# Token weights behind batch 0's inputs, fp32 filler matmuls and earlier u transposes in a fused scan and mixer

## The chip, the cores and the metric

The kernel runs on one core of one Trainium2 chip. Times are device microseconds (us) of that core. Most runs of a kernel agree within about one per cent; a run that is over 1.5% above the fastest of the same kernel is called slow and is left out of comparisons. The span of a profiled execution is about 2 us shorter than the device time of that execution (189.9 of 192.06 us for the kernel before), so spans are compared only with spans.

## The reference

```python
# recurrent part: B=4, H=8, S=768, D=48
state = alpha[t][:, None] * state + outer(k[t], v[t])
y[t]  = q[t] @ state
# y becomes x with shape (4, 768, 384); then a token and channel mixer
h  = relu(x^T @ w_tok1) @ w_tok2          # 768 -> 256 -> 768, over tokens
u  = x + h^T
h2 = relu(u @ w_ch1) @ w_ch2              # 384 -> 1536 -> 384, over channels
out = u + h2
```

Inputs and output are fp32; q, k, v and alpha come to 18.9 MB together.

## The kernel before

The sequence of each batch is cut into 6 chunks of 128 steps, so there are 24 chunks, n = 0 to 23. A chunk needs a logarithm of alpha, a cumulative sum on TensorE, two exponentials, products with k (GpSimd) and q (VectorE), transposes, scores, a mask product and the output y. When a batch's six chunks are done, its mixer runs: token products 1 and 2, u, transposes of u, 72 matmuls of channel product 1, and the same number of channel product 2. The mixer of one batch is interleaved with the chunks of the next.

A small scheduler of the program's own, `Plan`, simulates the engines with assumed durations and thereby fixes the order in which each engine gets its instructions. The chip then follows that order, whatever the real times are.

```python
class Plan:
    LAG = {"PE": 220, "ACT": 180, "DVE": 150, "POOL": 110}
    def op(self, engines, emit, deps=(), prio=0, takes=None, frees=(), lands=0.0): ...
    def issue(self):
        # ... takes the earliest possible operation, and of equals the lower prio
        slow = 2.0 if e == "PE" and start < self.cold else 1.0
        # ... models of the wire: `heavy` for weights, `wire` for inputs
        o["emit"](eng)

    inp = pool("inp", NIN)                                   # NIN = 6
    u128 = consts.tile([128, 128], BF16, name="u128")
    id128 = consts.tile([128, 128], BF16, name="id128")
    ones_col = consts.tile([128, 1], BF16, name="ones_col")
    # ... fix, wpool

    def load(n, name, src, after=None):                      # at, kt, qt, vt
            c[name] = inp.tile([128, H, D], F32, name=name)
            nc.sync.dma_start(c[name], src[b, :, ci * C : ci * C + C, :].transpose([1, 0, 2]))

    def weight(name, dst, src, after, us):                   # fp32 in DRAM, bf16 in SBUF
            gps.dma_start(dst, src)

    # state of the scan, in a ring of three buffers
    s_prev = ss_t[(n - 1) % NSS]                             # NSS = 3
    # e_ss (made for 5 of the 6 chunks of a batch) writes ss_t[n % NSS]

    for n in range(NT):                                      # NT = 24, NCH = 6
        # ... load_ak, load_qv, chunk(n)
        if n == NCH - 2:
            weight("wt1", wt1, src1, acqm, 2.6)
        if n == NCH - 1:
            weight("wt2", wt2, src2, pkk, 2.3)
            weight_ch1(0, vb); weight_ch1(1, vb); weight_ch1(2, vb)
        if n == NCH:
            weight_ch2(0, vb)
        if n == NCH + 1:
            weight_ch2(1, vb)
        # ... loads of chunk n + 1; mixer(b - 1) at the end of batch b
```

## Time and profile before

| | kernel before |
|---|---|
| device time, median of 3 runs | 193.34 us (192.79 to 193.99) |
| span of the profiled execution | 189.9 us (one of 192.06 us), mean granted clock 0.964 |
| TensorE busy | 168.6 us, 89% of the span |
| first matmul of channel product 1, batch 0 | 41.09 us |
| first and last matmul of channel product 2, batch 0 | 57.5 us and 75.5 us |
| last input used (logarithm of chunk 23) | 115.5 us |

The windows view of the kernel before gives for each stretch of time its length, the busy time and the number of instructions of TensorE (PE), its weight loads (PEld), VectorE (DVE), ScalarE (ACT) and GpSimd (POOL), the granted clock, the busy share of the DMA engines and the rate that they moved:

```profile
core 0: us, PE busy (x) PEld busy (x) DVE busy (x) ACT busy (x) POOL busy (x), PEclk, DMA share, GB/s
0.00:38.00 38.00, 23.36 (x238) 15.27 (x239) 19.77 (x42) 13.27 (x27) 16.16 (x34) 0.82 1.02 179
5.00:20.00 15.00, 9.70 (x111) 6.84 (x111) 10.31 (x14) 6.92 (x16) 6.98 (x12) 1.00 1.13 218
20.00:30.00 10.00, 5.50 (x70) 3.80 (x69) 5.44 (x9) 2.27 (x5) 5.86 (x10) 0.65 0.96 150
30.00:45.00 15.00, 14.08 (x102) 8.02 (x103) 7.12 (x13) 5.91 (x13) 2.54 (x5) 0.78 1.06 184
38.00:58.00 20.00, 19.42 (x189) 12.14 (x188) 10.26 (x18) 15.54 (x34) 9.35 (x14) 1.00 1.15 205
58.00:78.00 20.00, 20.00 (x236) 13.04 (x235) 13.04 (x20) 8.58 (x20) 11.17 (x18) 1.00 1.01 199
78.00:118.00 40.00, 37.33 (x480) 25.56 (x479) 27.98 (x44) 29.46 (x65) 24.94 (x39) 1.00 1.01 212
```

TensorE has no gap in 58 to 78 us, and gaps of 2.7 us in 78 to 118 us. In 20 to 30 us it is busy 5.50 of 10 us, and in 30 to 45 us it is busy but on average at 0.78 of its clock. The DMA share adds up the times of the packets on 16 engines, and so it can exceed 1.

The timeline of the kernel before shows start and duration, engine, line, operation, what is written and read, and in brackets the idle time before it and what ended that. Here are chunk 5's q product and the first of the channel matmuls:

```profile
28.03 0.56 DVE L283 TENSOR_TENSOR pkq_126<-qt,a_sb 128x384 bf16<-128x384 f32 x1 [2.46 <-DMA qt<-in_q_dram]
```

```profile
41.09 2.11 PE L474 MATMUL ps_mm<-ut,wc_156 128*128 128x384 bf16 x12 [0.28 <-DVE ut L455]
```

### The profile page before, as it was taken

What the parts mean: (1) busy time and instruction counts of PE and PEld (TensorE: products, weight loads), DVE (VectorE), ACT (ScalarE), POOL (GpSimd) and SP (SyncE); (2) the same over time, 40 slices, a digit from 0 to 9 for tenths busy, and PEclk for the clock granted to TensorE, in tenths of its full rate; (3) what the DMA queues carried; (4) which work ended last, traced back from release to release, by engine and by line L of the source; (5) the groups of instructions that cost most, each with busy time, mean ns of one, the idle gap of its engine ahead of it and who ended that gap; (6) DMA issues with size and microseconds to landing.
All of it is one profiled execution on the core that took longest, in us unless ns stands there. A gap on an engine that the chain in (4) does not pass through costs nothing.

```text
span 189.9 us, 4180 instructions
## 1 busy us (share of the span) xinstructions
PE 168.6 (89%) x1616; PEld 107.5 (57%) x1616; DVE 90.9 (48%) x152; ACT 93.7 (49%) x200; POOL 64.2 (34%) x108
## 2 busy tenths in 40 slices
PE   1377467989999999999979999999999999999992
PEld 0255344456666666657736676655665666566651
DVE  2378547172725676669734896323717102220222
ACT  3534411339885333677777588400664990059000
POOL 3643546006925555795535655500000000000000
PEclk9999955699999999999999999999999999999999
DMA  6999799999999999999999997022200001220122
GB/s 124 226 204 216 143 175 146 198 182 224 191 217 197 195 221 195 200 237 210 243 228 208 190 198 159 2 83 86 83 0 3 0 0 61 104 87 0 59 107 85
DMA packets 107139, 27.00 MB, mean 142 GB/s; under 512 B 100336, under 2 KB 107120, under 8 KB 107120
## 3 DMA queue, kind: packets, MB, share of 16 engines
q1 hardware_dynamic: 103296, 23.60, 58.1%
q0 software_dynamic: 3824, 3.15, 11.1%
q8 instruction: 12, 0.20, 0.4%
q14 instruction: 7, 0.06, 0.1%
HBM read 25.17 MB, written 4.72 MB: 157 GB/s over the span
## 4 chain that ended last, share of the span: by engine, by line
PE 70%; SPq 11%; DMA 8%; issue 3%; POOL 3%; DVE 2%; ACT 2%; POOLq 0%; DVEq 0%; ACTq 0%
PE ps_mm L492 25%; PE ps_mm L474 21%; SPq L230 11%; PE ps_mm L402 5%; PE ps_mm L426 4%; DMA qt<-in_q_dram 3%; PE gt_ps L324 3%; DMA vt<-in_v_dram 2%; DMA at<-in_alpha_dram 2%; PE ps_y L362 2%; PE ps_tp L307 2%; PE ps_mm L447 2%; PE ps_tp L312 2%; PE ps_y L367 1%; POOL pkk_131 L279 1%
## 5 line engine op out<-in xcount | busy, mean ns | idle before, releaser
L384 ACT ACTIVATE rt<-ps_mm 128x384 bf16<-128x384 f32 x90 | 43.2, 491 | 30.2 <-PE ps_mm L474 29.6
L474 PE MATMUL ps_mm<-ut,wc_156 128*128 128x384 bf16 x288 | 54.4, 326 | 0.3 <-DVE ut L455 0.3
L492 PE MATMUL ps_mm<-wc_157,rt 128*128 128x384 bf16 x288 | 49.7, 326 | 0.0
L492 PEld LDWEIGHTS <-rt 128*128 128x128 bf16 x288 | 27.3, 98 | 17.3 <-issue 0.2
L330 DVE TENSOR_TENSOR gtm<-gt_ps,u_107 128x1024 bf16<-128x1024 f32 x24 | 29.3, 1221 | 10.8 <-PE gt_ps L324 10.8
L474 PEld LDWEIGHTS <-wc_156 128*128 128x128 bf16 x288 | 25.9, 97 | 14.8 <-issue 0.8
L504 DVE TENSOR_TENSOR o_sb<-ps_mm,u_sb 128x384 f32<-128x384 f32 x24 | 13.4, 556 | 42.2 <-PE ps_mm L492 41.3
L317 DVE COPY tp<-ps_tp 128x1024 bf16<-128x1024 bf16 x21 | 14.4, 688 | 14.1 <-PE ps_tp L312 13.1
L291 POOL CAST vb<-vt 128x384 bf16<-128x384 f32 x24 | 12.1, 504 | 25.3 <-DMA vt<-in_v_dram 19.4
L375 ACT ACTIVATE x_sb<-ps_y 128x384 bf16<-128x384 f32 x24 | 11.8, 490 | 14.0 <-PE ps_y L367 13.8
L270 ACT ACTIVATE ia_sb<-ps_cum 128x384 f32<-128x384 f32 x24 | 11.8, 491 | 11.7 <-PE ps_cum L264 11.7
L433 DVE TENSOR_TENSOR u_sb<-ps_mm,x_sb 128x384 bf16<-128x384 f32 x24 | 11.8, 550 | 5.2 <-PE ps_mm L426 5.2
L402 PE MATMUL ps_mm<-x_sb,wt_154 128*128 128x384 bf16 x48 | 12.3, 375 | 0.0
L275 ACT ACTIVATE a_sb<-ps_cum 128x388 f32<-128x388 f32 x24 | 11.9, 495 | 0.0
L426 PE MATMUL ps_mm<-ht,wt_155 128*128 128x384 bf16 x48 | 10.6, 328 | 0.6 <-DVE u_sb L433 0.3
L279 POOL TENSOR_TENSOR pkk_131<-kt,ia_sb 128x384 bf16<-128x384 f32 x6 | 6.3, 1048 | 14.2 <-ACT ia_sb L270 14.2
L324 PE MATMUL gt_ps<-tp 48*128 48x128 bf16 x192 | 10.4, 233 | 0.6 <-DVE tp L317 0.4
L362 PE MATMUL ps_y<-vb,gtm 128*128 128x48 bf16 x192 | 9.3, 189 | 1.4 <-DVE gtm L330 1.4
L362 PEld LDWEIGHTS <-gtm 128*128 128x128 bf16 x192 | 8.2, 100 | 3.4 <-DVE gtm L330 2.0
L324 PEld LDWEIGHTS <-tp 48*128 48x128 bf16 x192 | 6.0, 99 | 6.2 <-issue 3.7
L279 POOL TENSOR_TENSOR pkk_130<-kt,ia_sb 128x384 bf16<-128x384 f32 x6 | 6.0, 997 | 8.8 <-ACT ia_sb L270 8.8
L279 POOL TENSOR_TENSOR pkk_129<-kt,ia_sb 128x384 bf16<-128x384 f32 x6 | 6.0, 1002 | 5.5 <-ACT ia_sb L270 5.5
(105 smaller groups left out, 195.5 us busy)
## 6 DMA issues: line engine op xcount, KB each, us to landing
at<-in_alpha_dram SPq DMA_DIRECT2D x24, 192.0 KB, 3.7
kt<-in_k_dram SPq DMA_DIRECT2D x24, 192.0 KB, 3.9
qt<-in_q_dram SPq DMA_DIRECT2D x24, 192.0 KB, 3.8
vt<-in_v_dram SPq DMA_DIRECT2D x24, 192.0 KB, 3.8
out_dram<-o_sb SPq DMA_DIRECT2D x24, 192.0 KB, 1.9
wc_156<-in_moe_w_ch_dram POOLq DMA_DIRECT2D x3, 384.0 KB, 5.9
wc_157<-in_moe_w_ch_dram POOLq DMA_DIRECT2D x2, 576.0 KB, 7.8
wt_154<-in_moe_w_tok_dram POOLq DMA_DIRECT2D x1, 384.0 KB, 6.6
```

Of the source, the lines that this page charges most:

```text
L230: nc.sync.dma_start(c[name], src[b, :, ci * C : ci * C + C, :].transpose([1, 0, 2]))
L279: gps.tensor_tensor(pkk_t[n % NPK][:, :, 0:D], c["kt"], c["ia"], ALU.mult)
L317: (dve.tensor_copy if e == "DVE" else act.copy)(c["tp"], c["ptp"])
L324: pe.matmul(gt[:, 4 * (h % 2) + j, :], lhsT=c["tp"][base : base + D, 4 + j, :], rhs=c["tp"][base : base + D, j, :], start=True, stop=True)
L330: dve.tensor_tensor(c["gtm"], c["gt"], mask_b, ALU.mult)
L362: pe.matmul(ps[:, h, :], lhsT=c["gtm"][:, 4 * (h % 2) + h // 2, :], rhs=c["vb"][:, h, :], start=(h == 0), stop=(ci == 0 and h == H - 1), s ...
L384: act.activation(dst, ps, AF.Relu)
L402: pe.matmul(hold["ps"], lhsT=wt1[:, kc, m * 128 : (m + 1) * 128], rhs=xs[b * NCH + kc], start=(kc == 0), stop=(kc == NS - 1), skip_group_c ...
L426: pe.matmul(hold["ps"], lhsT=wt2[:, kc, i * 128 : (i + 1) * 128], rhs=ht[kc], start=(kc == 0), stop=(kc == NDT - 1))
L474: pe.matmul(hold["ps"], lhsT=wc1[:, kc, mc * 128 : (mc + 1) * 128], rhs=ut_t[0][:, kc, cs], start=(kc == 0), stop=(kc == NM - 1))
L492: pe.matmul(hold["ps"], lhsT=rt[mc][:, i * 128 : (i + 1) * 128], rhs=wc2[:, mc, :], start=(mc == 0), stop=(mc == NDC - 1), skip_group_chec ...
L504: dve.tensor_tensor(hold["o"], hold["ps"], u[i], ALU.add)
```

## The change

The intent is to get batch 0's last chunks, and thus its mixer, started earlier. The first token weight is issued behind chunk 5's work rather than beside its inputs. TensorE's waits in the plan, between 19 and 36.5 us, are filled with matmuls of a constant fp32 tile whose result nobody reads, meant to keep the clock up. The u transposes get a higher priority. Some durations in the plan are refitted. The ring of states is indexed by the number of states made.

```diff
@@ Plan @@
+            if eng == "PE" and self.fill_from < start < self.fill_until:
+                idle = start - max(free[eng], self.fill_from)
+                warm = start > self.cold
+                for _ in range(int(idle * (0.75 if warm else 0.95) / (240.0 if warm else 450.0))):
+                    self.fill()
... (models of the wire: 2900 -> 2400, 1650 -> 1950, partial overlap, a lull; the plan's end of the slow clock: 36 -> 26 us)
@@ kernel @@
+    psy = ps_y_p.tile([128, 512], F32, name="ps_y")
+    def keep_busy():
+        pe.matmul(psy[:, HD:512], lhsT=u32, rhs=u32, start=True, stop=True,
+                  skip_group_check=True)
     u128 = consts.tile([128, 128], BF16, name="u128")
     make_upper_triangular(nc, u128, val=1.0, diag=True)
+    held = consts.tile([128, 1], F32, name="held")
+    u32 = consts.tile([128, 128], F32, name="u32")
+    dve.memset(u32, 1.0)
     id128 = consts.tile([128, 128], BF16, name="id128")
... 
+            if behind is not None:
+                gps.tensor_copy(held, behind["ia"][:, 0, 0:1])
             gps.dma_start(dst, src)
... (channel weights: 2.2 -> 2.8 us, 3.6 -> 4.7 us; RATE 205 -> 214)
... (cum, ia, a, pkk: priority P -> P - 0.3; u transposes and copies: TOK -> TOK - 0.3)
-        s_prev = ss_t[(n - 1) % NSS]
+        s_prev = ss_t[(n - 1 - b) % NSS]
-                    ss_t[n % NSS], ...
+                    ss_t[(n - b) % NSS], ...
         if n == NCH - 2:
-            weight("wt1", wt1, src1, acqm, 2.6)
+            loads[n]["qt"]["lull"] = 1300.0
+            early = vb
         if n == NCH - 1:
-            weight("wt2", wt2, src2, pkk, 2.3)
+            weight("wt1", wt1, src1, ia, 3.4, tiles[n])
+            ia["users"].append((wload["wt1"], None))
+            weight("wt2", wt2, src2, early, 2.9)
```

More of the change, by code (lines that the diff above doesn't have):

```diff
@@ L24, with __init__ @@
     LAG = {"PE": 220, "ACT": 180, "DVE": 150, "POOL": 110}
-    def __init__(self, rings, cold, window, slack):
+    def __init__(self, rings, cold, window, slack, fill, fill_from, fill_until):
+        self.fill, self.fill_from, self.fill_until = fill, fill_from, fill_until
         self.rings = rings
@@ L37, in op @@
         o = {"eng": engines, "emit": emit, "deps": [d for d in deps if d is not None],
-             "prio": (prio, len(self.ops)), "takes": [takes] if isinstance(takes, str) else list(takes or ()), "lands": lands, "users": [],
+             "prio": (prio, len(self.ops)), "takes": [takes] if isinstance(takes, str) else list(takes or ()), "lands": lands, "lull": 0.0, "users": [],
              "end": None}
@@ L57, in issue @@
                 at = max((d["end"] for d in o["deps"]), default=0.0)
-                if "PE" in o["eng"] and at > self.cold:
+                if "PE" in o["eng"] and at > self.fill_until:
                     at = max(d["end"] + (0.0 if "PE" in d["eng"] else self.slack)
@@ L83, in issue @@
             todo.remove(o)
+            if eng == "PE" and self.fill_from < start < self.fill_until:
[3 more added lines that the diff above has]
+                    self.fill()
             free[eng], o["start"] = done, start
             if o["lands"] and eng == "POOL":
-                first = max(heavy, start + 2900.0)
+                first = max(heavy, start + 2400.0)
                 heavy = first + o["lands"]
@@ L90, in issue @@
                 for p in self.ops:
-                    if p["lands"] and p is not o and (p["end"] or 0.0) > first + 900.0 and "SP" in p["eng"]:
-                        p["end"] += o["lands"]
+                    over = (p["end"] or 0.0) - 700.0 - first
+                    if p["lands"] and p is not o and over > 0.0 and "SP" in p["eng"]:
+                        p["end"] += o["lands"] * min(1.0, over / p["lands"])
             elif o["lands"]:
-                wire = max(wire, start + 1650.0) + o["lands"]
-                o["end"] = wire + 900.0
+                wire = max(wire, start + 1950.0) + o["lands"] + o["lull"]
+                o["end"] = wire + 700.0
             else:
@@ L138 @@
     NAUX, NGT, NRT, NMIX = 4, 3, 24, 3
+    FILL_FROM, COLD, FILL_UNTIL = 19000.0, 26000.0, 36500.0
     consts = pool("consts")
@@ L160 @@
                  "gtm": NGT, "ss": NSS, "x": 18, "ht": 4, "u": 12, "ut": 2, "rt": NRT,
-                 "o": 6, "pcum": 1, "ptp": 1, "pgt": 1, "py": 1, "pmix": NMIX}, 36000.0, {"PE": 0.0}, 600.0)
+                 "o": 6, "pcum": 1, "ptp": 1, "pgt": 1, "py": 1, "pmix": NMIX}, COLD, {"PE": 0.0}, 600.0,
+                keep_busy, FILL_FROM, FILL_UNTIL)
     act.preload_act_table_set("natural_log_exp_and_others")
@@ L194, with weight @@
     wload = {}
-    def weight(name, dst, src, after, us):
+    def weight(name, dst, src, after, us, behind=None):
         def emit(e):
+            if behind is not None:
+                gps.tensor_copy(held, behind["ia"][:, 0, 0:1])
             gps.dma_start(dst, src)
@@ L208, in weight_ch1 @@
         cs = slice(g * W1C, g * W1C + W1C)
-        weight(f"wc1{g}", wc1[:, :, cs], src3[:, :, cs], after, 2.2)
+        weight(f"wc1{g}", wc1[:, :, cs], src3[:, :, cs], after, 2.8)
     def weight_ch2(g, after):
         cs = slice(g * W2C, g * W2C + W2C)
-        weight(f"wc2{g}", wc2[:, cs, :], src4[:, cs, :], after, 3.6)
-    RATE = 205.0
+        weight(f"wc2{g}", wc2[:, cs, :], src4[:, cs, :], after, 4.7)
+    RATE = 214.0
     xs = {}
@@ L265, in e_cum @@
                           rhs=ones_col, start=True, stop=True, skip_group_check=True)
-        cum = plan.op({"PE": 260}, e_cum, [ln], P, takes="pcum", frees=[ln])
+        cum = plan.op({"PE": 260}, e_cum, [ln], P - 0.3, takes="pcum", frees=[ln])
         def e_ia(e):
@@ L270, in e_ia @@
             act.activation(c["ia"].rearrange("p h d -> p (h d)"), c["cum"][:, 0:HD], AF.Exp, scale=-1.0)
-        ia = plan.op({"ACT": 375}, e_ia, [cum], P, takes="ia", frees=[cum])
+        ia = plan.op({"ACT": 375}, e_ia, [cum], P - 0.3, takes="ia", frees=[cum])
         def e_a(e):
@@ L275, in e_a @@
             act.activation(c["a"], c["cum"][:, 0 : HD + 4], AF.Exp)
-        a = plan.op({"ACT": 375}, e_a, [cum], P, takes="a", frees=[cum])
+        a = plan.op({"ACT": 375}, e_a, [cum], P - 0.3, takes="a", frees=[cum])
         def e_pkk(e):
             gps.tensor_tensor(pkk_t[n % NPK][:, :, 0:D], c["kt"], c["ia"], ALU.mult)
-        pkk = plan.op({"POOL": 960}, e_pkk, [l_kt, ia], P, takes="pkk", frees=[l_kt, ia])
+        pkk = plan.op({"POOL": 960}, e_pkk, [l_kt, ia], P - 0.3, takes="pkk", frees=[l_kt, ia])
         def e_pkq(e):
@@ L351, in e_ss @@
                 dve.tensor_tensor(
-                    ss_t[n % NSS], c["s"][:, 0:HD].rearrange("p (h d) -> p h d", h=H),
+                    ss_t[(n - b) % NSS], c["s"][:, 0:HD].rearrange("p (h d) -> p h d", h=H),
                     bass.AP(tensor=m.tensor, offset=m.offset,
@@ L359, in e_y @@
         def e_y(e):
-            ps = c["y"] = ps_y_p.tile([128, H, D], F32, name="ps_y")
+            ps = c["y"] = psy[:, 0:HD].rearrange("p (h d) -> p h d", h=H)
             for h in range(H):
@@ L376, in chunk @@
         xop[n] = plan.op({"ACT": 375}, e_x, [y], P, takes="x", frees=[y])
-        return pkk, vb, acqm
+        return pkk, vb, acqm, ia
     xop = {}
@@ L448, in e_utp @@
                                      u[2 * g + i][:, j * 128 : (j + 1) * 128], id128)
-            tj = plan.op({"PE": 330}, e_utp, us[2 * g : 2 * g + 2], TOK,
+            tj = plan.op({"PE": 330}, e_utp, us[2 * g : 2 * g + 2], TOK - 0.3,
                          takes="pmix" if g else ["pmix", "ut"])
@@ L457, in e_ut @@
                     hold["ps"].rearrange("p (j i) t -> p j (i t)", i=2))
-            uts.append(plan.op({"DVE": 470, "ACT": 700}, e_ut, [tj], TOK,
+            uts.append(plan.op({"DVE": 470, "ACT": 700}, e_ut, [tj], TOK - 0.3,
                                frees=[(tj, "pmix")]))
@@ L516 @@
             load_qv(n)
-        pkk, vb, acqm = chunk(n)
+        pkk, vb, acqm, ia = chunk(n)
         if n == NCH - 2:
-            weight("wt1", wt1, src1, acqm, 2.6)
+            loads[n]["qt"]["lull"] = 1300.0
+            early = vb
         if n == NCH - 1:
-            weight("wt2", wt2, src2, pkk, 2.3)
+            weight("wt1", wt1, src1, ia, 3.4, tiles[n])
+            ia["users"].append((wload["wt1"], None))
+            weight("wt2", wt2, src2, early, 2.9)
             weight_ch1(0, vb)
```

## The prediction

> **What bounds it now.** Device time 193.34 us, profiled span 189.9 us. From 50 us on TensorE is nearly saturated: busy time by stretch is 10.00 of 10 us in 50–60, 60–70 and 70–80, 17.6 of 20 in 80–100, 19.7 of 20 in 100–120. The loss lies before the first channel matmul, at 41.09 us (timeline). DMA brings inputs until about 118 us, but TensorE then still has over 60 us of backlog.
>
> Two delays act before 41 us. (1) Batch 0's last q and v: issued at 21.7 and 22.4 us, used at 28.03 and 28.85; the chain of waits has 6.26 us of DMA for that q. The token weight issued at 21.36 us shares the wire: chunk 4's and 5's q and v and that weight are about 1.57 MB in 7.1 us (220 GB/s). VectorE's queue stands behind that q product, so chunk 4's mask product runs at 29.06, though its scores were done at 27. (2) The granted clock is 0.50 from 22.9 to 36.6 us: a 384-column matmul starts every 0.32 us instead of 0.16, and the first token product (31.5–36.2 us) runs wholly so. [...]
>
> **What the change does.** The first token weight goes behind batch 0's last chunk (about 23.5 us instead of 21.4), its data following the inputs. Without that 0.79 MB, the last q and v should land near 25–26 us, 2.5–3 us earlier. The token weights land later (estimate 30 and 33 us instead of 28 and 31.2), just in time. Added: five unread fp32 matmuls, two ahead of chunk 4's y, one before the last token-1 matmuls, two before token-2. [...] With the earlier inputs TensorE should be full from about 28 us, the clock back by 26–33 us. Half of the cold chain from 30 to 36.6 us, at most 3 us, can be saved, overlapping with (1). The earlier u transposes, and a first channel matmul that needs two of three of them, take about 0.5 us more off.
>
> I expect the first channel matmul at about 38.0 us (37–39.5), 3 us earlier. Later the orders change, not the work; saved time survives where TensorE is saturated. Part may go in 80–100 us, where chunk work follows input arrival (2.4 us idle now); earlier channel matmuls could also fill it. Net −3.3 us.
>
> **Predicted: 190.0 us**, 80% range 187.2 to 192.9. Faster by over 2% 0.38, within 2% 0.58, slower by over 2% 0.04.
>
> **Signs.** Right: chunk 5's q product by 26 us; clock 1.0 by 33 us; first channel matmul near 38; the shift still there at the end of batch 1's channel products and at the end. Wrong: clock low until 36 us; token matmuls waiting for weights; idle TensorE at 75–100 us grown by 2–3 us.
>
> **What would make it wrong.** [...] the fixed orders may misjudge when batch 1's inputs land and block on a late tile; or the new order removes more of the 6–7 us that TensorE loses after 41 us (then over 2%).

The forecast's sum came to −3.3 us, from 193.34 to 190.0 us: 3 us at the first channel matmul, and 0.3 us that it does not itemise. The fp32 matmuls had been put within waits.

## More of the kernel before

An input load brings 128 partitions of 8 heads times 48 fp32 values, so it is made of packets of 192 bytes, eight to a partition: the trace of the kernel before holds 98,304 packets of 192 bytes, which is 1,024 for each of the 96 input loads.

In 5 to 20 us, when only inputs are on the wire, 218 GB/s are 17,031 packets of 192 bytes, and 1.13 times 16 engines times 15 us is 271 us: 15.9 ns per packet.

The page's list of DMA issues ends each line with the median time from issue to landing:

```profile
at<-in_alpha_dram SPq DMA_DIRECT2D x24, 192.0 KB, 3.7
```

## The result, and the profile after

| | before | after |
|---|---|---|
| device time, median of 4 runs | 193.06 us (192.62 to 193.99) | 201.38 us (200.93 to 204.38) |
| span of the profiled execution | 189.9 us | 202.4 us |
| first channel-1 matmul, batch 0 | 41.09 us | 41.07 us |
| channel product 2 of batch 0, first and last matmul | 57.5 and 75.5 us | 60.0 and 79.3 us |
| logarithm of chunk 23 | 115.5 us | 125.2 us |

The ratio is 1.042, with a 95% interval of 1.0376 to 1.0464: the change costs 4.2%. Ratios are computed as the mean time of one kernel's fast runs over that of the other's of the same rounds, and so are not quite the ratio of the medians that are quoted. The profiled execution of the kernel after was a slow one of 204.38 us; its fast runs have spans of 198.9 to 199.6 us.

The windows view of the kernel after, for the stretches that were shown of the kernel before:

```profile
core 0: us, PE busy (x) PEld busy (x) DVE busy (x) ACT busy (x) POOL busy (x), PEclk, DMA share, GB/s
5.00:20.00 15.00, 8.73 (x93) 5.92 (x94) 8.04 (x10) 6.21 (x14) 6.98 (x11) 1.00 1.41 187
...
38.00:58.00 20.00, 18.73 (x167) 11.40 (x165) 10.35 (x17) 14.43 (x32) 9.34 (x14) 1.00 1.20 182
58.00:78.00 20.00, 17.31 (x191) 11.53 (x192) 9.85 (x15) 6.82 (x16) 8.25 (x13) 1.00 1.16 189
78.00:118.00 40.00, 34.33 (x428) 22.95 (x426) 23.72 (x33) 25.87 (x59) 22.72 (x35) 0.96 1.14 196
```

The first line is the finding. Already in 5 to 20 us, before the first token weight or filler, the same input loads move at 187 GB/s instead of 218, with a higher share of the DMA engines. By the same estimate as before a packet takes 23.2 ns instead of 15.9. The loss goes on: in 78 to 118 us TensorE is busy 34.33 of 40 us instead of 37.33. For scale, 18.9 MB take 87 us at 218 GB/s and 101 us at 187, an estimate from these two lines; chunk 23's input was seen used 9.7 us later.

The timeline of the kernel after, for chunk 4's and 5's q product, for the last scores of batch 0, which come before the clock rises, and for the first channel matmul:

```profile
26.85 1.05 DVE L304 TENSOR_TENSOR pkq_129<-qt,a_sb 128x384 bf16<-128x384 f32 x1
27.82 0.55 DVE L304 TENSOR_TENSOR pkq_130<-qt,a_sb 128x384 bf16<-128x384 f32 x1
```

```profile
32.46 0.61 PE L345 MATMUL gt_ps<-tp 48*128 48x128 bf16 x8
...
41.07 0.65 PE L495 MATMUL ps_mm<-ut,wc_160 128*128 128x384 bf16 x3 [0.27 <-DVE ut L476]
```

Chunk 5's product, which the prediction had put by 26 us, is at 27.82 us. The scores' eight matmuls take 0.61 us, as at 14.35 us in the kernel before; there they take 0.40 us at 17.47 us, at full clock. So TensorE is still slow at 32.46 us, although the windows view has 1.00 for the clock: the first clock record here is at 34.28 us and raises the clock, and before it the view shows 1.00. In the kernel before the first is at 16.08 us, and the same eight matmuls at 14.35 us were slow under a shown 1.00 too. It is safer to read the clock from the duration of a known matmul.

From the page of the kernel after, the chain that ended last, by engine and by line, and the DMA issue that answers to the one above; then TensorE's waits in 45 to 190 us (in total, times, longest):

```profile
PE 48%; DMA 27%; SPq 7%; issue 7%; POOL 6%; ACT 3%; DVE 0%; POOLq 0%; ACTq 0%
PE ps_mm L513 22%; PE ps_mm L495 15%; DMA at<-in_alpha_dram 13%; SPq L251 7%; DMA kt<-in_k_dram 7%; DMA wc_161<-in_moe_w_ch_dram 5%; DMA wt_159<-in_moe_w_tok_dram 2%; PE ps_mm L423 2%; PE gt_ps L345 1%; POOL vb L312 1%; PE ps_mm L447 1%; PE ps_tp L328 1%; PE ps_mm L468 1%; PE ps_y L383 1%; POOL pkk_133 L300 1%
...
at<-in_alpha_dram SPq DMA_DIRECT2D x24, 192.0 KB, 4.6
```

```profile
PE ps_cum L282 <- ACT la_128 L276: 2.8, 2, 1.6
PE ps_mm L513 <- DMA wc_161<-in_moe_w_ch_dram: 1.8, 1, 1.8
PE ps_cum L282 <- ACT la_125 L276: 1.6, 1, 1.6
PE ps_cum L282 <- ACT la_126 L276: 1.4, 1, 1.4
```

An alpha tile now lands 4.6 us after its issue, not 3.7. In the kernel before, DMA has 8% of that chain (not 27%), and TensorE's waits for logarithms come to 0.7 us in the same stretch, here 5.8. The logarithms (line 276) themselves wait for alpha. The lines of the kernel after are those of before plus 21 in this part.

### The profile page after: what moved, and what is told of

Its sections match the earlier page's. It is cut to its first block, busy times and chain, and to the rows that moved or that the text cites. A ratio compares the mean times of both kernels' runs of the same rounds, so it can differ in the third digit from the quotient of the medians.

```text
span 202.4 us, 4203 instructions
## 1 busy us (share of the span) xinstructions
PE 174.9 (86%) x1626; PEld 112.2 (55%) x1626; DVE 91.9 (45%) x152; ACT 94.3 (47%) x201; POOL 65.5 (32%) x109
## 2 busy tenths in 40 slices
DMA packets 107139, 27.00 MB, mean 133 GB/s; under 512 B 100336, under 2 KB 107120, under 8 KB 107120
## 4 chain that ended last, share of the span: by engine, by line
PE 48%; DMA 27%; SPq 7%; issue 7%; POOL 6%; ACT 3%; DVE 0%; POOLq 0%; ACTq 0%
PE ps_mm L513 22%; PE ps_mm L495 15%; DMA at<-in_alpha_dram 13%; SPq L251 7%; DMA kt<-in_k_dram 7%; DMA wc_161<-in_moe_w_ch_dram 5%; DMA wt_159<-in_moe_w_tok_dram 2%; PE ps_mm L423 2%; PE gt_ps L345 1%; POOL vb L312 1%; PE ps_mm L447 1%; PE ps_tp L328 1%; PE ps_mm L468 1%; PE ps_y L383 1%; POOL pkk_133 L300 1%
## 5 line engine op out<-in xcount | busy, mean ns | idle before, releaser
L495 PE MATMUL ps_mm<-ut,wc_160 128*128 128x384 bf16 x288 | 56.4, 334 | 0.4 <-DVE ut L476 0.3
L495 PEld LDWEIGHTS <-wc_160 128*128 128x128 bf16 x288 | 26.5, 100 | 16.0 <-issue 2.2
L291 ACT ACTIVATE ia_sb<-ps_cum 128x384 f32<-128x384 f32 x24 | 11.8, 493 | 16.6 <-PE ps_cum L285 16.5
L338 DVE COPY tp<-ps_tp 128x1024 bf16<-128x1024 bf16 x19 | 13.0, 686 | 12.6 <-PE ps_tp L333 12.6
L345 PE MATMUL gt_ps<-tp 48*128 48x128 bf16 x192 | 11.0, 243 | 1.7 <-DVE tp L338 1.6
L423 PE MATMUL ps_mm<-x_sb,wt_158 128*128 128x384 bf16 x48 | 11.4, 342 | 0.3 <-ACT rt L405 0.3
```

The lines of the kernel that those rows point to most:

```text
L338: (dve.tensor_copy if e == "DVE" else act.copy)(c["tp"], c["ptp"])
L345: pe.matmul(gt[:, 4 * (h % 2) + j, :], lhsT=c["tp"][base : base + D, 4 + j, :], rhs=c["tp"][base : base + D, j, :], start=True, stop=True)
L423: pe.matmul(hold["ps"], lhsT=wt1[:, kc, m * 128 : (m + 1) * 128], rhs=xs[b * NCH + kc], start=(kc == 0), stop=(kc == NS - 1), skip_group_c ...
L495: pe.matmul(hold["ps"], lhsT=wc1[:, kc, mc * 128 : (mc + 1) * 128], rhs=ut_t[0][:, kc, cs], start=(kc == 0), stop=(kc == NM - 1))
```

## Theories

Where could a slower wire come from at 5 us? The number of packets, 107,139, and the bytes are the same. What did change is where tiles lie. The built program's table of allocations (not a view of the profile) shows it: `held` takes 32 bytes of each partition and `u32` takes 512. Everything allocated behind them has moved by 544 bytes, which is 17 times 32. The input tiles start at byte 56,512 before, a multiple of 64, and at 57,056 after, which is 32 above one.

- *Placement*: the moved input tiles slow the input loads. It has two forms. In one (T1a below), packets that cross a 256-byte boundary cost more. In the other (T1b), packets whose starts aren't multiples of 64 do. Both are guesses that the runs below test.
- *Order*: the new order, or the fillers, cost time by themselves.
- *Lead given back*: once placement is mended, the 3 us gained before the first channel matmul are lost again later, to the wire or to late channel weights.
- *Chance*: the time of the first channel matmul differs from one execution to the next.

The first four kernels below (e1 to e4) were timed on one chip, e5 to e8 on a second, e9 to e12 on a third and e13 to e16 on a fourth; ratios are always to the kernel before on the same chip. The profiled executions of e1 to e8 and e10 to e16 are fast ones, and that of e9 is a single run whose state is unknown.

The texts below number these theories as they came up; each text says what its theories expect.

## The experiments

### Placement: the kernel after moved by another 32 bytes

```diff
-    held = consts.tile([128, 1], F32, name="held")
+    held = consts.tile([128, 16], F32, name="held")[:, 0:1]
```

> The changed kernel with nothing changed but 32 more bytes in its constants (the 4-byte tile that orders the token weight is given 64 bytes), so that all later tiles start at a multiple of 64 bytes again, as before, and not 32 bytes past one. T1 (placement: every input packet lands 32 bytes off in on-chip memory and that slows the input DMA from the first load on): input rate between 5 and 20 us back from 187 to 210-225 GB/s, time 188 to 191 us, that is the 3 us gain that was predicted, ratio to before 0.975-0.99. T2 (the new order and the fixed guesses of arrival cost the time): 199 to 202 us. T3 (the fp32 matmuls cost it): 199 to 202 us.

Measured: 196.09 us (194.08 to 196.53, 4 runs), the kernel before 194.7 us on that chip; ratio 1.0074 (0.9996 to 1.0152). The order of the instructions is untouched, yet 3.4% are gone: 1.042 over 1.0074 is 1.034. The windows view and the timeline of this run:

```profile
0.00:38.00 38.00, 26.28 (x265) 18.09 (x266) 21.90 (x48) 14.80 (x28) 17.16 (x35) 0.91 1.05 187
5.00:20.00 15.00, 10.80 (x111) 7.42 (x111) 8.97 (x13) 7.18 (x16) 8.11 (x13) 1.00 1.09 215
38.00:58.00 20.00, 18.12 (x178) 11.38 (x178) 9.17 (x13) 14.54 (x33) 9.33 (x14) 1.00 1.12 200
58.00:78.00 20.00, 17.97 (x185) 11.72 (x184) 8.50 (x14) 7.20 (x16) 9.31 (x15) 0.91 0.96 186
78.00:118.00 40.00, 37.41 (x476) 25.25 (x475) 28.66 (x44) 27.48 (x62) 24.67 (x40) 1.00 0.96 203
```

```profile
37.93 0.65 PE L495 MATMUL ps_mm<-ut,wc 128*128 128x384 bf16 x3 [0.27 <-DVE ut L476]
...
60.66 1.44 PE L513 MATMUL ps_mm<-wc,rt 128*128 128x384 bf16 x6 [2.03 <-DMA wc<-in_moe_w_ch_dram]
```

The rate is 215 GB/s again (15.6 ns per packet), and the first channel matmul is at 37.93 us, where the prediction had it. But the time isn't better than before: this theory's 188 to 191 us did not come. TensorE is 2.0 us short of full in 58 to 78 us, with 2.03 us of waiting for the second half of the channel-2 weight in it, and after that wait the clock is at half from 61.36 to 64.78 us.

### Placement: the kernel before moved by 32 bytes

```diff
-    ones_col = consts.tile([128, 1], BF16, name="ones_col")
+    ones_col = consts.tile([128, 32], BF16, name="ones_col")[:, 0:1]
```

> The kernel before with nothing changed but 32 more bytes in its constants, so that all later tiles lie 32 bytes past a multiple of 64. Same instructions in the same order. T1: input rate between 5 and 20 us falls from about 218 to about 187 GB/s, time 200 to 205 us, ratio 1.035-1.06. T2 and T3: 193 us, ratio 1.00.

Measured: 199.68 us (198.62 to 199.88), ratio 1.026 (1.0189 to 1.0332). A tile that is 31 columns wider and does nothing else makes the kernel before 2.6% slower. The windows view of this run:

```profile
5.00:20.00 15.00, 9.57 (x99) 6.60 (x98) 8.24 (x11) 6.52 (x14) 6.70 (x11) 1.00 1.44 188
```

Shorter stretches of the same run, in which only inputs are on the wire, show something that the averages hide:

```profile
2.00:4.50 2.50, 0.04 (x1) 0.04 (x1) 0.00 (x1) 0.54 (x2) 0.44 (x2) 1.00 1.09 203
8.00:10.00 2.00, 0.87 (x8) 0.71 (x8) 1.19 (x2) 0.00 (x0) 1.62 (x3) 1.00 1.43 187
82.00:84.00 2.00, 0.20 (x3) 0.12 (x2) 0.85 (x1) 1.29 (x3) 0.81 (x2) 1.00 1.18 219
111.00:113.00 2.00, 1.96 (x29) 1.52 (x29) 1.29 (x3) 1.41 (x5) 1.43 (x3) 1.00 1.30 186
```

By the same estimate a packet takes 16.5, 23.5, 16.6 and 21.5 ns in them. So the moved tiles do not slow every packet, and not the first ones. The packet records of the traces, averaged directly, say the same of all three kernels with moved tiles: 15.6 to 16.4 ns in 2 to 4.5 us and 23.3 to 23.6 ns in 8 to 10 us (the kernel after, this one and the next), against 15.2 to 15.7 and 15.2 to 15.9 ns in four profiles with 64-byte starts (the kernel before twice, e1 and e3). In the moved kernels the time climbs within about 3 us of dense loads (in the kernel after 16.3 ns in 4.5 to 5 us, 20.2 in 5 to 5.5 us and 23.0 in 7 to 8 us) and is low again after a stretch in which the loads were thin (16.6 ns in 82 to 84 us of this run). What this second condition is was not tested.

### Placement: the input tiles alone

The shift moved every tile behind it. To see which matter, two small pools go around the pool of input tiles. The first moves it by 32 bytes, and the second rounds this to 64, so that what follows keeps its phase.

```diff
+    padA = pool("padA")
+    padA.tile([128, 16], BF16, name="padA")
     inp = pool("inp", NIN)
+    padB = pool("padB")
+    padB.tile([128, 16], BF16, name="padB")
```

> The kernel before with only the four kinds of input tiles 32 bytes past a multiple of 64; weights, other operands and output tiles start at multiples of 64. If placement acts through the input DMA alone: input rate about 188 GB/s from 5 to 20 us and ratio 1.02-1.035, as e2. If it acts through weights, outputs or engine operands: ratio 1.00-1.01 and about 218 GB/s.

Measured: 200.1 us (199.11 to 200.38), ratio 1.0349 (1.0282 to 1.0416). The input tiles alone bring a loss as large as that of the run before. The windows view of this run:

```profile
5.00:20.00 15.00, 9.50 (x97) 6.58 (x97) 8.23 (x11) 6.44 (x14) 6.70 (x11) 1.00 1.43 187
```

### Placement: packets that never cross 256 bytes

Each head's 48 values get 64 columns (256 bytes), and the pool starts at a multiple of 256, so each 192-byte packet stays within one 256-byte block.

```diff
-    ones_col = consts.tile([128, 1], BF16, name="ones_col")
+    ones_col = consts.tile([128, 48], BF16, name="ones_col")[:, 0:1]
-                c[name] = inp.tile([128, H, D], F32, name=name)
+                c[name] = inp.tile([128, H, 64], F32, name=name)[:, :, 0:D]
... (the same where the first tile of batch 1 is made)
```

> The kernel before with each head's 48 input values given 64 places in on-chip memory (256 bytes, tile start a multiple of 256), so that no 192-byte packet crosses a 256-byte boundary on the writing side; before, two of four do (starts 0, 64, 128, 192), in the changed kernel three of four (32, 96, 160, 224). T1a ([...]): rate between 5 and 20 us rises well above before's, 240 to 320 GB/s, time below 190 us unless the fixed order blocks. T1b (only 64-byte starts matter): rate as before, about 218 GB/s, time within 1% of 193.

Measured: 194.5 us (192.6 to 194.7), ratio 0.999 (0.9917 to 1.0064). The rate is 211 GB/s, and not the 240 to 320 that the text gives for T1a, which was the author's estimate. By the estimate above, a packet takes 15.4 ns here (share 1.06, 211 GB/s), 15.9 ns before and 23.2 ns after. Of four packets none crosses a 256-byte boundary here, two do before and three after: crossing none instead of two made a packet only 0.5 ns quicker, crossing three made it 7.3 ns slower, and so the first form of the placement theory falls. The second form fits as far as it goes: layouts whose packets start 0, 64, 128 and 192 bytes above a multiple of 256 are fast in 5 to 20 us, and those whose packets start 32, 96, 160 and 224 above one are slow there. It is not the whole of it, because the first packets of the moved kernels were fast too (above). Why was not found; it is a dependence that was measured, not a mechanism.

This run also starts its channel product early, at 37.3 us against 41.1, with the order of the kernel before. The windows view of it, and what GpSimd waited for in 44 to 60 us and TensorE in 38 to 60 us:

```profile
5.00:20.00 15.00, 11.22 (x112) 7.81 (x113) 9.09 (x13) 7.06 (x16) 7.00 (x13) 1.00 1.06 211
38.00:58.00 20.00, 16.26 (x159) 9.93 (x158) 6.67 (x10) 13.95 (x33) 9.46 (x14) 1.00 1.10 190
58.00:78.00 20.00, 20.00 (x239) 13.15 (x237) 13.19 (x19) 8.65 (x21) 10.84 (x17) 1.00 1.03 202
78.00:118.00 40.00, 37.50 (x471) 25.45 (x470) 28.15 (x43) 28.89 (x65) 25.29 (x39) 1.00 1.02 214
```

```profile
POOL pkk L279 <- DMA kt<-in_k_dram: 4.0, 1, 4.0
```

```profile
PE ps_tp L307 <- POOL pkk L279: 2.9, 1, 2.9
```

It has lost its lead by 58 us: TensorE is busy 16.26 of 20 us in 38 to 58 us, where the profile of the kernel before had 19.42. TensorE waits 2.9 us for a k product, and GpSimd waits 4.0 us for the k tile. That TensorE is ahead does not make batch 1's inputs come earlier.

### The fillers left out

```diff
     def keep_busy():
-        pe.matmul(psy[:, HD:512], lhsT=u32, rhs=u32, start=True, stop=True,
-                  skip_group_check=True)
+        pass
```

This is on top of the mended placement (`held` 16 wide), as is every run from here on whose base is the kernel after.

> The changed kernel at 64-byte starts, without the five fp32 matmuls, all else in the same order. If the fp32 matmuls hold or bring back the clock as meant: clock 0.5 for longer around 30-37 us and 1 to 3 us slower than the run with them. If the earlier inputs alone do it: the same time within 0.5 us, or up to 1 us faster.

Measured: 194.7 us (194.02 to 197.12), ratio 1.0011 (0.9944 to 1.0077), against 1.0074 with fillers: not told apart. The clock does answer to them. In the profiles of the five versions with mended placement, real inputs and fillers (e1, e8, e11, e13, e14) it came back at 29.80 to 30.64 us, and in the three without fillers (e4, e12, e15) at 33.68 to 34.60 us. The first channel matmul is at 37.1 to 38.4 us in the five and at 38.9 to 39.0 us in the three. That is one execution each, but the two groups do not overlap, so the fillers did what they were meant to do; the gain of about 1 us did not reach the end.

### Input packets eight times as long

The input loads read contiguous memory, 1,536 bytes to a partition, instead of the right eight pieces. The result is wrong. It tells what each order would do with a faster wire.

```diff
-            nc.sync.dma_start(c[name], src[b, :, ci * C : ci * C + C, :].transpose([1, 0, 2]))
+            nc.sync.dma_start(c[name], src[b].rearrange("h s d -> (h s d)")[ci * C * HD : (ci + 1) * C * HD]
+                              .rearrange("(p h d) -> p h d", p=C, h=H))
```

> Wrong result on purpose: the kernel before, but each input load of 196,608 bytes reads one contiguous piece of the tensor (1,536 bytes to a partition instead of eight packets of 192), same bytes, same instructions, same order. T4 (from about 57 us on the end is set by the arrival of the inputs: in all six profiles the last chunk's log of alpha is taken 74 to 77 us before the end, whatever went before; a lead of TensorE over the inputs is given back): inputs arrive much earlier, the end moves with TensorE's own work, 178-187 us. Rival T5 (TensorE is saturated after 50 us, inputs matter only at the start): 3 to 6 us off before's time, only what the start saves.

> Wrong result on purpose: the same fast loads in the changed kernel at 64-byte starts. T4: with the inputs no longer the limit the earlier first channel matmul shows in the total, so this run is 1 to 4 us faster than e5_before_fast. If it is as slow as or slower than e5_before_fast, the new order itself costs TensorE time (or its gain at the start came only from waiting for inputs, which is gone here).

Measured: the order of before 188.96 us (187.23 to 190.59), ratio 0.9744 (0.9657 to 0.9831); the order of after 194.41 us (193.8 to 196.58), ratio 1.0017 (0.9937 to 1.0097). With the inputs at 266 GB/s in 5 to 20 us the order of before gains 2.6%, and the new order gains nothing. On this chip and with this wire, the new order is 2.8% slower than the old (1.0017 over 0.9744). The order of before starts its channel product at 33.94 us here, 3 to 7 us earlier than in its four profiles with real inputs (37.3 to 41.1 us), and ends about 5 us earlier: a lead lasts better where the inputs keep up. It is the 3 to 6 us of the rival T5, though, and not the 178 to 187 us of T4. TensorE's waits in 38 to 80 us, first with the order of before, then with the new one:

```profile
PE ps_mm L492 <- DMA wc<-in_moe_w_ch_dram: 3.1, 1, 3.1
```

```profile
PE ps_mm L513 <- DMA wc<-in_moe_w_ch_dram: 5.7, 2, 3.0
```

When inputs are quick, the channel-2 weight becomes the next thing to wait for. It is issued at 43.0 us at the latest in the first and at 49.1 us in the second, because the plan puts it behind GpSimd's work for chunks 6 and 7. During these waits the granted clock falls to half, from 54.77 to 58.18 us in the first and from 55.28 to 68.93 us in the second. No fast-wire version with this weight issued earlier was run, so the 2.8% may come from the weight's place and not from the rest of the order.

### Batch 0's stores held back

If the lead is lost to the wire, keeping the six stores of batch 0 (issued at 79 to 97 us in the kernel before) off it until all inputs have been issued should help.

```diff
+    stores = []
-            plan.op({"SP": 650}, e_st, [o], -1, lands=196608 / 350.0, frees=[o])
+            stores.append(plan.op({"SP": 650}, e_st, [o], -1, lands=196608 / 350.0, frees=[o]))
...
+    for st in stores[:NS]:
+        st["deps"].append(loads[NT - 1]["vt"])
```

> The kernel before, with batch 0's six output stores issued behind the last input load in the one queue that carries both (they are ready at 79-96 us; six output buffers hold them; the next batch's outputs begin at 121 us). Their 1.18 MB and the waits of the queue for their results are then out of the way of the inputs. T4: the last inputs arrive about 4 to 6 us earlier and the end follows, 187 to 190 us. T5: 193 us, no change.

> The same stores behind the loads, in the changed kernel at 64-byte starts. T4: 4 to 7 us faster than e1, 188 to 191 us. T5: as e1, 196 us.

> e8 repeated on another chip, as the base of the next three (64-byte starts, batch 0's stores behind the loads): ratio 0.988-1.000.

Measured: in the kernel before 194.24 us, ratio 0.9991 (0.9941 to 1.0041). In the kernel after 193.16 us (192.39 to 193.85), ratio 0.9931 (0.9873 to 0.9989), which looked like a gain; the same kernel again on another chip, with six runs, had 195.29 us and 1.0044 (0.9998 to 1.009). The gain did not repeat. The stores aren't what takes the lead.

### The kernel before, unchanged

> The kernel before once more, for a second profile of it. T7 (the stretch at half clock before the first channel matmul is chance: [...] the total doesn't care): the first channel matmul anywhere between 37 and 42 us, the end within 1.5% of 192-194 us all the same. Rival: first channel matmul again at 41.1 us within 0.3.

Measured: one look, 194.19 us, span 192.4 us. In this execution of the unchanged kernel the first channel matmul was at 38.66 us rather than 41.09, as this timeline of it shows, and yet the end came no earlier:

```profile
38.66 2.11 PE L474 MATMUL ps_mm<-ut,wc 128*128 128x384 bf16 x12 [0.28 <-DVE ut L455]
```

What GpSimd waited for in 44 to 60 us of this run:

```profile
POOL pkk L279 <- DMA kt<-in_k_dram: 3.5, 1, 3.5
POOL vb L291 <- DMA vt<-in_v_dram: 2.9, 1, 2.9
```

With the two runs above that change the layout (256 bytes to a head) or the stores, and neither of which touches the work before 38 us in any other way, the order of before starts its channel product at 37.3, 37.6, 38.7 and 41.1 us and channel product 2 at 58.0, 58.4, 60.3 and 57.5 us. The start is spread over 3.8 us, and it does not set what follows.

### The channel-2 weight earlier

```diff
         if n == NCH - 1:
...
             weight_ch1(2, vb)
-        if n == NCH:
             weight_ch2(0, vb)
-        if n == NCH + 1:
+        if n == NCH:
             weight_ch2(1, vb)
```

> The changed kernel at 64-byte starts, with each half of the second channel weight issued one step earlier in the queue (first half behind the first channel weight, second half behind chunk 6). T6 (what is left of the loss is that TensorE, early at the first channel product, waits for the second channel weight at 58.6-60.7 us [...]): no wait for that weight, clock 1.0 from 35 us on, ratio to before 0.98-0.995, that is 2 to 4 us better than e1. Rival (T4: inputs and weights together fill the wire until about 60 us and any lead is given back there): the wait moves to the inputs of chunks 6 to 9, ratio 1.00-1.01 as e1.

Measured: 193.71 us (192.97 to 195.22, 6 runs), ratio 1.0036 (0.9977 to 1.0096). The wait for that weight is gone: channel product 2 starts at 55.28 us, against 56.83 in the mended kernel after, and the timeline names no idle time before it. The clock stays full from 30.39 us to the last matmuls, too.

```profile
55.28 2.12 PE L513 MATMUL ps_mm<-wc,rt 128*128 128x384 bf16 x12
```

The time is still that of the kernel before. The waits in 60 to 120 us are 2.2 us for logarithms, which need alpha. Taking away the weight's wait leaves the inputs'.

### Both, with and without fillers

> e8 (64-byte starts, batch 0's stores behind the loads) without the five fp32 matmuls. If they are worth something: 0.3 to 1 us slower than e8 and a ratio over 0.995. If they only cost: ratio 0.985-0.993, as e8 or up to 1.5 us better.

> e13 and the second channel weight one step earlier (as e11). If the wait for that weight is a real cost: 1 to 3 us faster than e13, ratio 0.975-0.988, and faster than both kernels. If the lead is given back to the inputs' arrival: within 0.5% of e13.

> e14 without the five fp32 matmuls, same chip. Worth something: slower than e14 by over 0.5%. Cost: faster than e14 by over 0.5%. No matter (the clock before the first channel matmul doesn't reach the total): within 0.5%.

These combine the edits above: stores held back and no fillers (e12); stores held back and the weight early (e14); and all three (e15). Measured: 194.42 us (ratio 1.0057, 0.9994 to 1.012), 194.6 us (1.0015, 0.9968 to 1.0062) and 195.3 us (1.0051, 1.0006 to 1.0096). Leaving the fillers out goes from 1.0074 to 1.0011, from 0.9931 and 1.0044 to 1.0057, and from 1.0015 to 1.0051. The sign changes, so what the fillers are worth at the end was not resolved.

### The order of before with stores held back and the weight early

> The kernel before with the same two moves of DMA issues (stores behind the loads, second channel weight one step earlier). If the new order of the engines has a worth of its own once the wire is out of its way: 1 to 2% slower than e14. If not: within 0.5% of e14.

Measured: 196.15 us, ratio 1.0096 (1.0056 to 1.0137), and a wrong result that was not intended: its relative error is 0.0497. The order in which the program gives out its instructions explains it. States are made for five chunks of six, and the plan lets state 18 start when the state made three before it, state 14, is free. But `ss_t[n % NSS]` gives state 18 the buffer of state 15, and in this kernel the y of chunk 16, which reads state 15, is given out after state 18 is written. The trace agrees: state 18 is written at 101.58 us and the y of chunk 16 reads at 102.45 us; in the kernel before they are at 101.55 and 94.52 us. So the kernel before has a latent fault that its own order doesn't trigger, and the index `(n - b) % NSS` of the change mends it. No run with the mended index was spent on it. The time of a wrong kernel tells little about the order.

No version with the right inputs beat the kernel before by more than the spread of the runs.

## Why the prediction was wrong

The result, 201.38 us, lies far above the range of 187.2 to 192.9 us.

- **The list of costs left out placement.** "What the change does" counted the fp32 matmuls and the moved loads, and not that two constant tiles move every tile behind them. This was the step that failed most: undoing it alone takes 4.2% to 0.7%, and doing it alone to the kernel before costs 2.6%, or 3.5% to its input tiles alone. That the tiles move was readable from the diff, with the allocation table; what that would cost was not.
- **"Chunk 5's q product by 26 us."** Right with the placement mended: there the two products of chunks 4 and 5 run from 23.99 to 25.72 us. With the change as it stands it was 27.82 us.
- **"The clock back by 26–33 us."** 30.64 us with mended placement (29.80 to 30.64 in five versions with fillers, 33.68 to 34.60 in three without), 34.28 us as it stands, 36.56 us in the profile of before. The clock was at half from 22.91 to 36.56 us in the kernel before and from 23.82 to 30.64 us in the mended version; what sets these times, beyond the difference between versions with and without fillers, was not shown. The order of before began its channel product anywhere in 37.3 to 41.1 us.
- **"The first channel matmul at about 38.0 us."** Right in size: 37.93 us with mended placement, and 37.1 to 39.0 us in the seven other runs with it that keep the real inputs. But the 41.09 us that it was compared with was the latest of four executions of the order of before with real inputs in tiles that start at multiples of 64. Part of the 3 us was never there to be gained.
- **"Saved time survives where TensorE is saturated."** This failed, and it is why the mended version isn't faster. That "the loss lies before the first channel matmul" is the same error, and so is the size of "Net −3.3 us". From the windows of the mended version, TensorE is busy 2.9 us more by 38 us (26.28 against 23.36), 1.3 us less in 38 to 58 us and 2.0 us less in 58 to 78 us, and 0.1 us more in 78 to 118 us: a sum of −0.3 us. In 118 to 150 us it is another 1.1 us short (30.89 against 32.00). At 38 us work had been pulled ahead of the inputs of batch 1 and of the channel-2 weight. Of the waits that followed, 2.0 us were for that weight and 2.4 us for two logarithms whose alpha came late (before the matmuls at 102.80 and 119.11 us); 1.8 us in 38 to 58 us were for VectorE's work on the same chunk, after channel product 1 had been used up (its last matmul is at 52.97 us). That a TensorE which looks saturated was so because it had started late enough for its data to be there is the reading of these waits; it was not tested by itself. Busy time counts a slow clock's matmuls as longer (a 384-column one took 0.53 us at half clock and 0.32 us at full clock in the kernel before), and the two profiles are of executions of 196.03 and 192.06 us, so these sums are only a guide; the last matmul of channel product 2, at 78.0 us against 75.5 in batch 0 and at 134.7 against 132.4 in batch 1, says the same.
- **"Token matmuls waiting for weights"** did not come about, but the same warning holds for the channel-2 weight: 2.03 us of waiting in the mended version.
- **"Idle TensorE at 75–100 us grown by 2–3 us"**, named as a sign of failure, came in part: 1.5 us in that stretch (21.15 us busy against 22.62) and 3.0 us in 78 to 118 us of the kernel after. The wire, slower by placement, is enough to cause it: in 78 to 118 us the kernel before with moved tiles is busy 34.58 us (and 34.55 with the input tiles alone moved), the kernel after 34.33, and the mended version 37.41 against 37.33 of before. But one other mended version (e13, stores held back) had 34.85 us, so the new order can idle there too.
- **The fp32 matmuls' cost.** The prediction had put them within waits, with an estimate that is cut. In the kernel after two fillers took up 0.96 us, from 30.72 us to the next matmul, at the slow clock, and two took 0.58 us, from 36.69 to 37.27 us, at the full one: 0.48 us and 0.29 us each. The trace has two records to a filler.

What stays open: why loads into tiles that start 32 bytes above a multiple of 64 were slow (187 to 188 GB/s in 5 to 20 us, where seven profiles with starts at a multiple of 64 had 211 to 218), and what else it takes for that, since the first loads are not slow; what the fillers are worth at the end; and whether the few tenths of a per cent that the mended versions mostly have above the kernel before are a cost of the order or nothing, although with a faster wire the order did cost 2.8%. That the lead is given back is shown by the versions that start early and end alike. Which of the waits would have to go for it to last is only argued: with the weight's wait gone, and with the stores held back, it did not.

## What to carry to other kernels

When a small constant tile is added, compare the start addresses of all DMA destinations modulo 64 before and after, and pad the tile so that they stay: here a move by 32 bytes cost the kernel before 2.6% when every tile behind a constant moved, and 3.5% when only the input tiles did. A lead at one point is worth only as much as the data behind it come earlier too, so ask what each later product waits for once it is 3 us ahead (the mended version was so at 38 us, and ended at a ratio of 1.0074). Before a single profile's milestone is used as the baseline of a prediction, take a second profile of the same kernel.
